# Gate and up slices in pairs of 1,024 columns, row gradients in one run per partition, and another issue order

## The chip, the cores and the metric

One core of a Trainium2 chip runs the kernel. It has five engines with a queue each: TensorE (PE), VectorE (DVE), ScalarE (ACT), GpSimd (POOL) and SyncE (SP). Sixteen DMA engines move data between device memory (DRAM) and the on-chip memory of 128 partitions; here nearly all transfers are issued by SP. The metric is the device time in microseconds (us); the time before is the median of three runs.

## The reference

A decode step of a transformer block, forward and backward: attention over a cache and a gated MLP side by side, and the gradients of all their inputs. All tensors are bf16.

```python
def _A_ref(x, k_cache, v_cache, wq, wo):          # B=2, Sq=1, D=576, Hq=32, Hkv=16, Sk=4096, Dh=128
    ...
    scores = jnp.einsum("bhqd,bhkd->bhqk", q, k) * (Dh ** -0.5)
    p = _softmax(scores, axis=-1)
    o = jnp.einsum("bhqk,bhkd->bhqd", p, v)
    return (lambda x, *d: x.transpose(*d))(o, 0, 2, 1, 3).reshape(B, Sq, Hq * Dh) @ wo

def _B_ref(x, w_gate, w_up, w_down):              # F = 4608
    g = jnp.einsum("bsd,df->bsf", x, w_gate)
    u = jnp.einsum("bsd,df->bsf", x, w_up)
    h = g * u
    return jnp.einsum("bsf,fd->bsd", h, w_down)

xn = _layernorm(x, axis=-1)
return x + _A_ref(xn, A_k_cache, A_v_cache, A_wq, A_wo) + _B_ref(xn, B_w_gate, B_w_up, B_w_down)
...
_out, _vjp = jax.vjp(_f, A_x, A_k_cache, A_v_cache, A_wq, A_wo, B_w_gate, B_w_up, B_w_down)
_grads = _vjp(grad_out)
```

The outputs are out_0 (the block's result), out_1 (gradient of x), out_2 and out_3 (of the K and V caches), out_4 (wq), out_5 (wo), out_6 (gate), out_7 (up), out_8 (w_down). With two rows of x, each weight and cache element is read once and each gradient element written once, and every gradient is an outer product of few vectors.

## The kernel before

**Work.** Attention runs in 16 steps (8 groups of two K/V heads, two batches). A step loads K and V of two heads, 1 MB each (128 partitions x 8 KB), transposes them on DVE in 32x32 blocks (`turn`), computes scores and softmax on PE, ACT and DVE (`softmax`, `dscore`), contracts (`contract`), and forms the gradients of V (`out1`, to out_3) and K (`out0`, to out_2) in `head_outer`: outer products on PE into a PSUM tile `ps_o`, four casts by ACT or DVE (`cp`, lines 436 and 438) into a store slot, one store of 1 MB. Each group also loads a slice of wq and one of wo, and `group_back` writes their gradients. The MLP is cut into nine slices of `FS` = 512 of the 4,608 columns (`mlp`).

**Buffers.** Sixteen slots of 8 KB per partition (`big`) are shared by three users with a cap each: loaded K/V (`kv`, 8), transposed data (`X`, 13) and outgoing gradients (`st`, 4). Gate and up of one slice go into the one `gu` tile (9 x 512 columns: four row blocks of gate, four of up, and the last 64 rows of both). Five `ww` tiles hold slices of wq, wo and w_down. `tl` tiles hold the gradients of the last 64 of the 576 rows (tails).

**Transfers of a slice.** Gate and up each come as one transfer of 512 rows x 512 columns (line 1039: runs of 1,024 bytes) and one of the last 64 rows (line 1042), w_down in 4,608 bytes per partition (line 1046). The main gradients of gate and up (`cols_outer`, 512 KB, runs of 1,024 bytes) and wq go out likewise; those of w_down and wo (`rows_outer`, 576 KB) put row a·128+p on partition p, four runs of 1,152 bytes for each partition. A row unit is two matmuls (line 699), one for each of two row groups of 32, into the two banks of a `ps_o` tile.

**Order.** The whole program is generated ahead by a planner (`Order`). Each piece of work is a stream that asks for slots, engines and transfers with costs written into the source; the planner starts what can start first and breaks ties within a window (`SLACK`) by a priority from `pr`, which adds up the tables `PR`, `HEAD`, `TAIL` and `OFF` by name and step. `MLP_AT`, `WQ_AT` and `WO_AT` tell after which K/V load a weight load may be asked for. What runs on the chip is the resulting fixed order of instructions of each engine, with waits on semaphores where data or slots are needed; SP issues its transfers in that order too. At the end of the run `final_out` (lines 1345 to 1364) sums and stores out_0, and `final_dx` (lines 1376 to 1402) out_1.

Of the kernel before, what the change touches and what calls it, by code (L numbers as in the profile page):

```python
# [13 lines left out]
P = 128  # L14
# [282 lines left out]
NBIG, NGU, NWW, NBD = 16, 1, 5, 3  # L297
CAP = {"kv": 8, "X": 13, "st": 4}
OFF = {"mload": {2: 138.2, 8: 8.9}, "wload": {10: 3.1, 13: 2.1}, "BD1": {1: -144.5}, "out1": {4: 2.3, 6: -20.1,
       8: 2.5}, "W1": {4: 1.3, 7: -1.7}, "turn1": {4: -0.1, 5: -115.7, 11: -198.7}, "load": {1: 20.8, 10: -89.9,  # L300
       11: -16.3, 14: -4.1}, "front": {3: -111.8, 14: -87.3}, "turn0": {4: 6.0, 15: -118.8}, "con": {10: 3.3},
       "W0": {14: -1.6}, "back": {5: -15.0}}
MLP_AT = [0.93, 10.84, 15.91, 23.71, 30.89, 34.72, 45.87, 53.36, 60.85]
WQ_AT = [-1, 8, 16, 24, 32, 40, 48, 56]
WO_AT = [3, 7, 16, 26, 34, 40, 50, 58]
# [6 lines left out]
HEAD = {"turn0": -25.2, "turn1": -31.7, "att": -70.5, "dsc": 459.9, "con": 83.3, "out1": 26.9, "out0": 94.5,  # L312
        "front": 23.5, "back": -376.6, "W0": -16.3, "W1": 64.8, "BD1": 30.3, "BD0": 46.9, "conv": -75.9,
        "load": -114.3}
TAIL = {"turn0": 43.7, "turn1": 191.7, "att": 96.6, "dsc": 0.2, "con": -89.5, "conv": 36.8, "out1": -32.0,
        "out0": 229.2, "front": -529.0, "back": -358.1, "W1": 39.2, "BD1": -22.9, "BD0": -120.6, "load": 281.8}
PR = {"turn0": -84.8, "turn1": -109.1, "att": -681.0, "dsc": -731.0, "conv": 64.6, "con": -230.8, "out1": 1310.1,
      "out0": 250.5, "front": 164.9, "back": -70.9, "W0": -353.3, "W1": -31.6, "BD1": 442.2, "BD0": -91.5,
      "mlp": -130.5, "wout": -277.2, "store": 413.2, "load": 0.3, "wload": -718.4, "fin": 231.3, "const": 5.5,
      "mload": -58.3}  # L320
# [8 lines left out]
def kernel(  # L329
# [30 lines left out]
    G = 2  # L360
# [12 lines left out]
    HD2 = D // 2  # L373
    WB = 4 * FS + 256
# [277 lines left out]
    class Store:  # L652
        def __init__(self, n, out, prio):
            self.n, self.out, self.prio = n, out, prio

        def done(self):
            self.n -= 1
            if self.n == 0:
                yield SPAWN(self.out(), self.prio + PR["store"])

    def put(engine, parts, tag, slot, events=(), row=8192):
        def run():
            for j, (dst, src, nbytes) in enumerate(parts):
                yield DMA(engine, 0.36, nbytes, row)
                nc.sync.dma_start(dst, src)
            yield ("lrel", tag, slot)
            for e in events:
                yield SET(e)
        return run

    def unit(mms, pe, cols, ev, store, quad=None, kind="r"):
# [6 lines left out]
        yield from store.done()  # L678

    def cols_unit(A, rhs, st, off):  # L680
# [7 lines left out]
        def ev(e, o):  # L688
            cp(e, view(st[:], 0, P, off + 256 * A, [[P, 2], [FS, 4], [1, P]]),
               o[:].rearrange("p a (d f) -> p a d f", d=4))  # L690
        return mms, (0.213, 0.208), 1024, ev

    def rows_unit(j, lhs, st):
        A, k = divmod(j, 2)

        def mms(o):
            for aa in range(2):
                a = 2 * A + aa
                nc.tensor.matmul(o[:, aa, 0:HD2], lhsT=lhs(a), rhs=dyr[32 * a:32 * a + 32, k * HD2:(k + 1) * HD2],
                                 start=True, stop=True)  # L700
# [3 lines left out]
        return mms, (0.12, 0.052), D, ev  # L704

    def rows_outer(lhs, dst, p, events=()):
        i = yield ACQ("st")
        st = st_t[i]
        src = st[:, 0:FC * D].rearrange("p (h n) -> p h n", h=FC)
        store = Store(FC, put("SP", [(dst, src, 128 * FC * D * 2)], "st", i, events, 4608), p)  # L710
        for a in range(FC):
            yield SPAWN(unit(*rows_unit(a, lhs, st), store), p)

    def cols_outer(rhs, dst, p, events=()):
        i = yield ACQ("st")
        st = st_t[i]
        src = st[:, 0:4 * FS].rearrange("p (c n) -> p c n", n=FS)
        store = Store(2, put("SP", [(dst, src, 128 * 4 * FS * 2)], "st", i, events, 4096), p)
        for A in range(2):
            yield SPAWN(unit(*cols_unit(A, rhs, st, 0), store), p)  # L720

    def tail_outer(rhss, dsts, p, events=()):
        i = yield ACQ("tl")
        st = tl_t[i]
        nw = len(rhss)
        parts = [(d, st[64 * w:64 * w + 64, 0:FS], 64 * FS * 2) for w, d in enumerate(dsts)]
# [722 lines left out]
```

## Time and profile before

| | us |
|---|---|
| median of 3 runs | 485.66 |
| lowest, highest | 484.40, 486.44 |
| the profiled execution's own time | 484.63 |
| its span on the core (first to last instruction) | 482.8 |

The profile is a page about one execution. It gives for each engine the busy time and its share of the span, and for the DMA engines the packets (a packet is one contiguous run that one of the 16 engines moves), their bytes, and the time they took as a share of 16 engines' span. Packets may overlap a little, so a stretch can show a share slightly over 1. "PE" rows are matmuls and "PEld" rows weight loads; "128*32" is rows x columns of the array that a matmul occupies, and the shape after it is that of the moving data. A group row ends with the busy time and the mean of one in ns, and after the second bar with the idle time before them and what ended it. A row of stretches gives for each engine the busy time and the count, then the TensorE clock granted (1.00 is full), the DMA share and GB/s. "SPq" rows are the issues of transfers; their duration is that of issuing, not of moving.

### The profile page before, as it was taken

The numbers are of one execution on the slowest core, as the hardware profiler recorded it, in microseconds if no ns is written. First come the engines' busy times: TensorE is split into PE (matmuls) and PEld (weight loads), VectorE is DVE, ScalarE is ACT, GpSimd is POOL, SyncE is SP. The second block draws the span as 40 slices with busy tenths as digits, with TensorE's granted clock in tenths as the row PEclk, the third lists the DMA queues.
The fourth block names the chain that finished last, engine by engine and source line by source line (L and its number), as shares of the span: only waits on it lengthen the run. The fifth ranks groups of instructions, "written<-read, shape, count | busy, mean of one in ns | idle before, by whom it ended". The sixth has DMA issues, their size and how long they took to land.

```text
span 482.8 us, 14538 instructions
## 1 busy us (share of the span) xinstructions
PE 367.1 (76%) x6122; PEld 209.5 (43%) x6122; DVE 352.8 (73%) x667; ACT 345.9 (72%) x520; POOL 155.5 (32%) x220
## 2 busy tenths in 40 slices
PE   1447869877985998578797687856995878896986
PEld 1324535444452553245353353434452444443534
DVE  8679565996875888776857697768877777758672
ACT  6039279986876688667887788837875768896892
POOL 3140314563115403423414242253404451430600
PEclk9969585775665558777675579567565765757565
DMA  7999999999999999999999999999999999999985
GB/s 295 417 366 374 339 406 375 308 405 412 403 401 388 409 400 407 375 409 407 389 385 417 411 373 415 398 392 412 388 390 367 402 411 382 414 390 416 411 351 193
DMA packets 65266, 185.90 MB, mean 385 GB/s; under 512 B 4393, under 2 KB 47665, under 8 KB 48817
## 3 DMA queue, kind: packets, MB, share of 16 engines
q1 hardware_dynamic: 65192, 184.96, 99.2%
q8 instruction: 48, 0.79, 0.6%
q14 instruction: 18, 0.14, 0.1%
q10 hardware_dynamic: 8, 0.00, 0.0%
HBM read 92.48 MB, written 92.48 MB: 383 GB/s over the span
## 4 chain that ended last, share of the span: by engine, by line
DMA 58%; PE 17%; ACT 9%; DVE 8%; issue 4%; SPq 3%; DVEq 0%; ACTq 0%
DMA out_dram<-big 26%; DMA gu<-in_B_w_up_dram 12%; DMA gu<-in_B_w_gate_dram 9%; ACT big L436 8%; DMA ww<-in_A_wo_dram 7%; DVE big L432 5%; PE ps_o L1138 4%; DMA big<-in_A_v_cache_dram 3%; PE ps_m L1293 2%; PE ps_m L1116 2%; PE ps_m L779 2%; DMA ww<-in_B_w_down_dram 2%; SPq L1042 2%; DVE big L438 1%; PE ps_m L900 1%
## 5 line engine op out<-in xcount | busy, mean ns | idle before, releaser
L436 ACT CAST big<-ps_o 128x1024 bf16<-128x1024 f32 (+1 forms) x325 | 289.9, 961 | 39.0 <-PE ps_o L1138 28.8
L432 DVE STREAM_TRANSPOSE big<-big 128x1024 f32<-128x1024 f32 x128 | 153.6, 1222 | 16.0 <-DMA out_dram<-big 8.3
L1104 POOL TENSOR_TENSOR BD<-vr,mask 128x2048 bf16<-128x2048 bf16 x32 | 115.3, 3604 | 112.3 <-ACT vr L436 77.0
L438 DVE CAST big<-ps_o 128x1024 bf16<-128x1024 f32 (+1 forms) x51 | 56.0, 1097 | 10.2 <-PE ps_o L1138 4.1
L1116 PE MATMUL ps_m<-big,W 128*32 128x128 bf16 x2048 | 58.3, 279 | 4.5 <-POOL W L1081 1.7
L1138 PE MATMUL ps_o<-BD,pp 32*128 32x512 bf16 x256 | 50.6, 549 | 9.6 <-ACT big L436 6.4
L1116 PEld LDWEIGHTS <-W 128*32 128x32 bf16 x2048 | 46.6, 124 | 20.8 <-issue 16.4
L1138 PE MATMUL ps_o<-BD,dd 32*128 32x512 bf16 x256 | 46.5, 496 | 6.2 <-ACT big L436 5.3
L1081 POOL COPY W<-rep 32x16 bf16<-32x16 bf16 x128 | 24.6, 192 | 65.3 <-DVE rep L884 60.4
L636 POOL COPY wt<-wm 64x128 bf16<-64x128 bf16 (+1 forms) x34 | 8.9, 261 | 107.1 <-DVE wm L629 105.9
L432 DVE STREAM_TRANSPOSE big<-ww 128x1152 f32<-128x1152 f32 x25 | 34.1, 1365 | 7.6 <-DMA out_dram<-big 4.9
L1293 PE MATMUL ps_m<-big,pp 128*32 128x512 bf16 x256 | 31.4, 592 | 0.0
L761 PE MATMUL ps_m<-gu,xs 128*32 128x128 bf16 x360 | 11.1, 279 | 26.7 <-DMA gu<-in_B_w_gate_dram 17.3
L432 DVE STREAM_TRANSPOSE big<-gu 128x1024 f32<-128x1024 f32 x18 | 21.6, 1226 | 5.1 <-DMA out_dram<-big 5.1
L1293 PE MATMUL ps_m<-big,dd 128*32 128x512 bf16 x256 | 23.9, 457 | 1.0 <-DVE hb L785 0.7
L764 ACT COPY gs<-ps_m 128x256 f32<-128x256 f32 x9 | 3.5, 384 | 29.2 <-PE ps_m L761 29.2
L1138 PEld LDWEIGHTS <-pp 32*128 32x128 bf16 x256 | 11.1, 100 | 26.6 <-issue 22.9
L1138 PEld LDWEIGHTS <-dd 32*128 32x128 bf16 x256 | 10.7, 98 | 25.1 <-issue 18.3
L685 PEld LDWEIGHTS <-xnr 32*128 32x128 bf16 x416 | 15.9, 119 | 12.8 <-issue 12.0
L761 PEld LDWEIGHTS <-xs 128*32 128x32 bf16 x360 | 7.7, 121 | 30.9 <-DMA gu<-in_B_w_gate_dram 19.4
L685 PE MATMUL ps_o<-hb,xnr 32*128 32x128 bf16 x288 | 16.7, 281 | 3.4 <-ACT big L436 2.9
L766 DVE TENSOR_TENSOR hb<-gs,ps_m 128x128 bf16<-128x128 f32 x9 | 2.6, 285 | 19.8 <-ACT gs L764 19.8
(199 smaller groups left out, 513.2 us busy)
## 6 DMA issues: line engine op xcount, KB each, us to landing
out_dram<-big SPq DMA_DIRECT2D x64, 1024.0 KB, 12.2
big<-in_A_k_cache_dram SPq DMA_DIRECT2D x32, 1024.0 KB, 12.7
big<-in_A_v_cache_dram SPq DMA_DIRECT2D x32, 1024.0 KB, 11.9
out_dram<-big SPq DMA_DIRECT2D x26, 512.0 KB, 11.3
out_dram<-big SPq DMA_DIRECT2D x17, 576.0 KB, 8.9
ww<-in_B_w_down_dram SPq DMA_DIRECT2D x9, 576.0 KB, 8.3
ww<-in_A_wo_dram SPq DMA_DIRECT2D x8, 576.0 KB, 10.7
gu<-in_B_w_gate_dram SPq DMA_DIRECT2D x9, 512.0 KB, 15.3
```

Source lines behind the costliest of these rows:

```text
L432: nc.vector.transpose(out, in_)
L436: nc.scalar.copy(out, in_)
L438: nc.vector.tensor_copy(out=out, in_=in_)
L685: nc.tensor.matmul(o[:, aa, dc * P:(dc + 1) * P], lhsT=xnr[32 * a:32 * a + 32, dc * P:(dc + 1) * P], rhs=rhs(a), start=True, stop=True)
L761: nc.tensor.matmul(ug[32 * a:32 * a + 32, 1 - w, :], lhsT=xs[:, dc if dc < 4 else 4 + w, :], rhs=gu[:, FS * k + P * a:FS * k + P * (a + 1) ...
L779: nc.tensor.matmul(dh, lhsT=Wdy[:, e, 2 * k:2 * k + P], rhs=view(X[:], 0, P, 64 * k + e, [[D, FC], [2, 32]]), start=(k == 0 and e == 0), s ...
L1042: nc.sync.dma_start(gu[64 * w:64 * w + 64, 8 * FS:9 * FS], Wsrc[512:576, f0:f0 + FS])
L1081: nc.gpsimd.tensor_copy(view(W_t[t][w][:], 32 * a, 32, 6 + 8 * a, [[G * WW, 4], [WW, G], [1, 2]]), view(rep_t[grp[g]["qs"]][:], 32 * a, 32 ...
L1104: nc.gpsimd.tensor_tensor(BD_t[i][:], view(vr_t[v][:], 0, P, 0, [[0, 16], [1, Dh]]), view(mask16[:], 0, P, 0, [[1, 16], [0, Dh]]), ALU.mult)
L1116: nc.tensor.matmul(sc[32 * cq:32 * cq + 32, :], lhsT=view(W[:], 0, P, (be * G + l) * WW + 6 - 4 * c2 - 2 * l, [[1, 32]]), rhs=view(X[:], 0 ...
L1138: nc.tensor.matmul(o[:, k, :], lhsT=pr2[32 * c4:32 * c4 + 32, :], rhs=BD[32 * c4:32 * c4 + 32, 8 * l + 4 * h2:8 * l + 4 * h2 + 4, :], star ...
L1293: nc.tensor.matmul(ct[32 * j:32 * j + 32, :], lhsT=view(rT, 0, P, 4 * c + 2 * l, [[1, 32]]), rhs=kv_t[kvS[s][t][l]][:, Dh * c:Dh * (c + 4) ...
```

## The change

It does four things. (1) Gate and up are loaded for two slices at once, 1,024 columns, each weight into one slot of the shared ring (new user `G`, cap 2); the `gu` tile keeps only the 64-row tails. The ninth slice stays alone. The two slices of a pair are still computed one by one. (2) The main gradients of gate and up of a pair fill one store slot for each weight, half by half, and leave in one transfer of 1 MB. (3) The row gradients (w_down and wo) are laid out with rows 4p to 4p+3 on partition p: a run of 4,608 bytes per partition. For that a row unit takes 8 matmuls of 32x32 in place of 2 of 32x128. (4) The planner's numbers are new: `kv` 7 for 8, `X` 12 for 13, six `ww` tiles for five, another cost for some transfers, and new tables throughout, so nearly every engine's order differs. The order of SP's transfers, which can be read from the built programs, has 252 transfers for 276.

```diff
 def DMA(engine, cost, nbytes, row=8192):
-    packet = 0.0364 * row + 8.0
+    packet = 0.0364 * row + 8.7
...
-NBIG, NGU, NWW, NBD = 16, 1, 5, 3
-CAP = {"kv": 8, "X": 13, "st": 4}
+NBIG, NGU, NWW, NBD = 16, 1, 6, 3
+CAP = {"kv": 7, "X": 12, "st": 4, "G": 2}
...
-LM, LAG = 0.16, 1.39
+LM, LAG = 0.15, 1.75
...
-SLACK = {"PE": 0.1, "ACT": 0.11, "DVE": 0.43, "POOL": 0.47, "SP": 17.19}
+SLACK = {"PE": 0.08, "ACT": 0.3, "DVE": 0.46, "POOL": 24.94, "SP": 1554.58}
...
-    kv_t = X_t = st_t = tiles("big", NBIG, [P, NCH * Dh])
+    kv_t = X_t = st_t = G_t = tiles("big", NBIG, [P, NCH * Dh])
...
-    gu_t = tiles("gu", NGU, [P, 9 * FS])
+    gu_t = tiles("gu", NGU, [P, 2 * FS])
...
+    def put(dst, src, nbytes, row, tag, slot, ready):
+        yield WAIT(*ready)
+        for d, x in zip(dst, src):
+            yield DMA("SP", 0.36, nbytes, row)
+            nc.sync.dma_start(d, x)
+        yield ("lrel", tag, slot)
...
-    def rows_unit(j, lhs, st):
+    def rows_unit(j, t, st):
...
             for aa in range(2):
-                a = 2 * A + aa
-                nc.tensor.matmul(o[:, aa, 0:HD2], lhsT=lhs(a), rhs=dyr[32 * a:32 * a + 32, k * HD2:(k + 1) * HD2],
-                                 start=True, stop=True)
+                for q in range(4):
+                    nc.tensor.matmul(o[32 * q:32 * q + 32, aa, 0:HD2], lhsT=view(t, 32 * q, 32, 2 * A + aa, [[4, 32]]),
+                                     rhs=dyr[32 * q:32 * q + 32, k * HD2:(k + 1) * HD2], start=True, stop=True)
...
+    def rows_outer(t, dst, p, event):
         i = yield ACQ("st")
+        st, done = st_t[i], events(FC)
+        yield SPAWN(put([dst.rearrange("(p c) n -> p (c n)", c=FC)], [st[:, 0:FC * D]], 128 * FC * D * 2, 4608,
+                        "st", i, done), p + PR["store"])
+        for j in range(FC):
+            yield SPAWN(unit(*rows_unit(j, t, st), done[j]), p)
...
+    def cols_store(i, dst, width, done):
+        return put([dst.rearrange("(c p) n -> p c n", p=P)], [st_t[i][:, 0:4 * width].rearrange("p (c n) -> p c n", n=width)],
+                   128 * 4 * width * 2, 2 * width, "st", i, done)
...
+    def cols_half(sl, hh, w, rhs, p, event):
+        if hh == 0:
+            sl["st"][w] = i = yield ACQ("st")
+            dst = (out_6, out_7)[w][0:512, sl["f0"]:sl["f0"] + sl["width"]]
+            yield SPAWN(cols_store(i, dst, sl["width"], sl["done"][w]), p + PR["store"])
+            yield SET(sl["open"][w])
+        else:
+            yield WAIT(sl["open"][w])
+        done = sl["done"][w][2 * hh:2 * hh + 2]
+        for A in range(2):
+            yield SPAWN(unit(*cols_unit(A, rhs, st_t[sl["st"][w]], FS * hh, sl["width"]), done[A]), p)
...
+    def free_gu(sl):
+        yield WAIT(*sl["turned"])
+        for b in sl["G"]:
+            yield REL("G", b)
+        yield REL("gu", sl["gu"])
...
+                t, c0 = (main[w], width * dc + FS * hh) if dc < 4 else (gu, FS * hh)
                 for a in range(4):
...
+                                     rhs=t[:, c0 + P * a:c0 + P * (a + 1)], start=(dc == 0), stop=(dc == 4))
...
-        t32(pairs(X[:, 0:2048]), pairs(gu[:, 0:2048]))
...
+            t32(pairs(X[:, 2048 * w:2048 * (w + 1)]).rearrange("p (c n) -> p c n", c=4),
+                pairs(main[w][:, 0:4 * width]).rearrange("p (c n) -> p c n", c=4)[:, :, HFS * hh:HFS * (hh + 1)])
...
+            halves = range(2 * i, min(2 * i + 2, NFS))
+            f0, width = 2 * i * FS, FS * len(halves)
...
             for w, Wsrc in enumerate((B_w_gate, B_w_up)):
...
+                b = yield ACQ("G")
+                sl["G"].append(b)
+                yield DMA("SP", 0.4, 128 * 4 * width * 2, 2 * width)
+                nc.sync.dma_start(G_t[b][:, 0:4 * width].rearrange("p (c n) -> p c n", n=width),
+                                  Wsrc[0:512, f0:f0 + width].rearrange("(c p) n -> p c n", p=P))
+                yield DMA("SP", 0.36, 64 * width * 2, 2 * width)
+                nc.sync.dma_start(gu[64 * w:64 * w + 64, 0:width], Wsrc[512:576, f0:f0 + width])
```

More of the change, by code (lines that the diff above doesn't have):

```diff
@@ L315 @@
[L315 to L320, printed above, removed]
+HEAD = {"turn0": 358.0, "turn1": -88.8, "att": -420.1, "dsc": 372.9, "con": 241.2, "out1": -625.8, "out0": 80.7,
+        "front": 43.6, "back": 73.0, "W0": 584.4, "W1": -340.9, "BD1": 39.3, "BD0": 397.4, "conv": 284.3,
+        "load": 102.5}
@@ L650, in dxn, with unit @@
                                  start=(s == 0), stop=(s == St - 1))
[L652 to L671, printed above, removed]
+    def put(dst, src, nbytes, row, tag, slot, ready):
[4 more added lines that the diff above has]
+        yield ("lrel", tag, slot)
+    def unit(mms, pe, cols, ev, done, quad=None, kind="r"):
         i = yield ACQ("o")
@@ L677, in unit, with events, cols_unit @@
         yield REL("o", i)
-        yield from store.done()
-    def cols_unit(A, rhs, st, off):
+        yield SET(done)
+    def events(n):
+        return [Event() for _ in range(n)]
+    def cols_unit(A, rhs, st, off=0, width=FS):
         def mms(o):
@@ L740, in tail_outer, with mlp @@
         for A in range(2):
[L741 to L749 removed]
+            yield SPAWN(unit(*mk(A), done[A]), p)
+        yield WAIT(*done)
+        yield SET(event)
+    def free_gu(sl):
[3 more added lines that the diff above has]
+        yield REL("gu", sl["gu"])
+    def mlp(i, hh, sl, Lgu, Ld, wd_slot):
+        gu, wd = gu_t[sl["gu"]], ww_t[wd_slot]
+        main, width = [G_t[b] for b in sl["G"]], sl["width"]
         hs = yield ACQ("hb")
@@ L1144, in mk @@
             return mms, (0.213, 0.052), 1024, ev
-        def one(A, h2):
-            yield from unit(*mk(A, h2), store, A)
-            yield SET(done[2 * A + h2])
         for h2 in range(2):
             for A in range(2):
-                yield SPAWN(one(A, h2), pr(f"out{t}", s))
+                yield SPAWN(unit(*mk(A, h2), done[2 * A + h2], A), pr(f"out{t}", s))
     def outer(s, t, tag, slot, pr2):
```

144 lines of the change are left out of this document (73 added, 71 removed), and 11 rows, old and new, of the table OFF.

## The prediction

> **What bounds the kernel now.** I read the page first, then the busy time by stretches, the issue rows of SP, and the end of the run in order of time.
>
> ```profile
> span 482.8 us, 14538 instructions
> PE 367.1 (76%) x6122; PEld 209.5 (43%) x6122; DVE 352.8 (73%) x667; ACT 345.9 (72%) x520; POOL 155.5 (32%) x220
> ...
> DMA packets 65266, 185.90 MB, mean 385 GB/s; under 512 B 4393, under 2 KB 47665, under 8 KB 48817
> ...
> q1 hardware_dynamic: 65192, 184.96, 99.2%
> ...
> out_dram<-big SPq DMA_DIRECT2D x64, 1024.0 KB, 12.2
> big<-in_A_k_cache_dram SPq DMA_DIRECT2D x32, 1024.0 KB, 12.7
> big<-in_A_v_cache_dram SPq DMA_DIRECT2D x32, 1024.0 KB, 11.9
> out_dram<-big SPq DMA_DIRECT2D x26, 512.0 KB, 11.3
> out_dram<-big SPq DMA_DIRECT2D x17, 576.0 KB, 8.9
> ```
>
> The packets of SP's queue took 99.2% of sixteen engines' whole span, while no compute engine is above 76%. The kernel is bound by its transfers. Three quarters of the packets are under 2 KB, although the 128 K/V transfers of 1 MB (128 packets of 8 KB each) hold 134 of the 186 MB. So the time can fall in two ways: cheaper packets for the same bytes, or fewer moments with nothing to move. The next view gives both; its last two columns are the DMA share and GB/s.
>
> ```profile
> 5.00:15.00 10.00, 2.53 (x48) 1.51 (x48) 9.13 (x34) 4.33 (x7) 0.00 (x0) 1.00 1.02 426
> 27.50:29.50 2.00, 0.37 (x2) 0.10 (x1) 1.78 (x3) 0.60 (x2) 2.00 (x2) 0.54 1.10 304
> 47.00:49.00 2.00, 1.06 (x8) 0.94 (x9) 0.90 (x4) 1.11 (x4) 0.00 (x0) 0.79 1.04 360
> 58.00:60.50 2.50, 2.50 (x86) 1.58 (x76) 1.51 (x3) 1.73 (x3) 0.00 (x0) 0.92 1.09 348
> ...
> 3.00:483.00 480.00, 367.09 (x6122) 209.54 (x6122) 350.70 (x659) 344.52 (x519) 153.09 (x209) 0.67 1.00 387
> 38.00:54.00 16.00, 11.62 (x260) 8.28 (x250) 13.61 (x27) 11.47 (x20) 1.63 (x3) 0.82 0.92 342
> 72.00:98.00 26.00, 22.72 (x440) 14.31 (x441) 19.61 (x37) 23.75 (x35) 13.79 (x16) 0.63 0.98 347
> 458.00:470.00 12.00, 10.52 (x152) 4.41 (x150) 8.09 (x13) 11.21 (x15) 1.61 (x3) 0.64 0.90 349
> 476.00:483.00 7.00, 3.13 (x16) 1.54 (x14) 1.52 (x9) 0.41 (x1) 0.00 (x0) 0.50 0.14 43
> ```
>
> What each short stretch moves follows from the issues:
>
> ```profile
> 2.64 0.97 SPq L1005 DMA_DIRECT2D big<-in_A_k_cache_dram  x2
> ...
> 10.88 1.93 SPq L1039 DMA_DIRECT2D gu<-in_B_w_gate_dram  x1
> ...
> 17.36 15.12 DMA gu<-in_B_w_up_dram
> ...
> 39.06 8.79 SPq L665 DMA_DIRECT2D out_dram<-big  x5
> 48.35 1.80 SPq L665 DMA_DIRECT2D out_dram<-tl  x2
> ...
> 52.89 0.38 SPq L1039 DMA_DIRECT2D gu<-in_B_w_gate_dram  x1
> ```
>
> From 5 to 15 us the 1 MB K/V loads run: 426 GB/s with 8 KB packets. At 27.5 to 29.5 (the up weights land at 32.5) and 58 to 60.5 gate and up loads run in 1,024-byte rows: 304 and 348 GB/s. At 47 to 49 gradients are stored, in rows of 1,024 and 1,152 bytes: 360 GB/s. The engines are equally full in all four (share 1.02 to 1.10; packets overlap a little), so the rate falls with the row. Against that full share, three stretches ran partly dry: (1.02-0.92)x16 + (1.02-0.98)x26 + (1.02-0.90)x12 = 4.1 us. The last 7 us move almost nothing.
>
> **The packets, step by step.** The time of a packet on one of 16 engines is 16 x bytes / rate: 8,192 B take 307.7 ns; a 1,024 B load takes 47.1 (58 to 60.5) or 53.9 ns (27.5 to 29.5); a gradient packet of 1,024 B takes 45.5 ns, or, if all were 1,152 B, 51.2. Taking time = fixed + bytes x slope, the fixed part from the pair (8,192; 1,024) is (t - 307.7/8)/(7/8): 9.9 or 17.6 ns for loads, 8.0 to 9.2 for stores (the 1,152-byte pair likewise). The bytes do not change, so only the fixed part is saved, once per packet that goes away.
> - Gate, up and their main gradients: four pairs of slices, two weights; 1,024 packets become 512. 8 x 512 = 4,096 fewer in loads, 4,096 in stores. The ninth slice stays as it was.
> - The 64-row load tails of these pairs: 8 x 64 = 512 fewer. The tail stores stay.
> - Row gradients (the 17 stores of 576 KB above): 512 packets of 1,152 B become 128 of 4,608 B: 17 x 384 = 6,528 fewer.
>
> Loads 4,608 x 9.9 ns / 16 = 2.9 us, stores 10,624 x 8.0 / 16 = 5.3 us: **8.2 us**. Bounds: 7.6 us with 8.0 ns for all; 11.2 us with 17.6 and 9.2. I take the low ends because the 27.5 stretch has the highest overlap (1.10), so its price is partly a queue and not a packet. SP also issues 252 transfers in place of 276. At 16 end marks each (4,393 small packets / 276) that is 384 packets; at no more than the 8 ns fixed part, 0.2 us, left in the bounds.
>
> **What the edit adds.** Casts and transposes keep their number and elements; gate and up are now read in four runs per transpose. One wait grows: a pair's main gradient leaves SP after four casts, two from each half, where two were enough, and everything later in SP's order stands behind it.
>
> ```profile
> SPq L665 <- ACT big L436: 88.7, 53, 7.4
> ```
>
> SP waits 88.7 us for casts already, 7.4 at the longest, and the engines stay full, because transfers land 11 to 13 us after their issue and so some 4 MB are queued. A longer wait costs what it exceeds that cover; it is in the order's term below. The row gradients get new matmuls: 8 of 32x32 per unit where 2 of 32x128 stood, 68 units.
>
> ```profile
> L699 PE MATMUL ps_o<-dyr,R 32*128 32x288 bf16 x64 | 10.6, 376 | 2.7 <-ACT big L436 2.2 <-DVE big L438 0.3
> L699 PE MATMUL ps_o<-dyr,hb 32*128 32x288 bf16 x72 | 10.0, 335 | 4.8 <-ACT big L436 4.3 <-DVE big L438 0.2 <-DVE tl L438 0.2
> ...
> L1310 PE MATMUL ps_m<-fold,osb 128*128 128x4 bf16 x128 | 8.4, 170 | 3.1 <-ACT osb L1303 2.8
> ```
>
> A unit occupies PE for (10.6+10.0)/68 = 0.30 us now. A matmul with 4 columns lasts 0.17 us, so of 0.335 to 0.376 some 0.19 us is streaming. If four row groups run side by side, as two do now, a unit makes two rounds: about +0.2 us, 14 us over the run, inside PE's 116 us of idle time. If all eight take turns, a unit makes eight streams: +1.1 us. No row of before has four row groups writing one bank, so this stands between +0.2 and +1.1; I take +0.2 (L699 itself overlaps its two) and keep the other as a rival.
>
> **The order.** Both programs' issue orders can be read before they run, and they differ nearly everywhere. Three things bear on time.
> - The end. After the last row-gradient work, before runs out_0 and then out_1's chain on PE, one behind the other:
>
> ```profile
> 472.40 0.32 DVE L973 TENSOR_TENSOR accx<-accx,ps_m 128x160 f32<-128x160 f32 x1
> ...
> 472.83 1.87 PE L1359 MATMUL ps_o<-identf,acc 128*2 128x64 f32 x16
> 474.62 0.37 PE L1362 MATMUL ps_o<-identf,acc 64*2 64x64 f32 x2
> ...
> 480.21 0.41 ACT L1337 CAST xy<-ps_o 2x320 bf16<-2x320 f32 x1 [4.77 <-PE ps_o L1400]
> ```
>
> The new order has out_0's 18 matmuls ahead of the last evictions and the L643 group ahead of the last column unit. From 472.26 to 474.99 that is 2.7 us out of the chain that ends the run. The four row units at the end give back 4 x 0.2 = 0.8. Together **-1.9 us**, between 0 (the last store decides instead) and -2.7.
> - The gaps. They could all be filled (-4.1). Against that stand new long bursts: the longest row of stores without a load is 9.1 MB (before 5.5), and a dry queue is more likely there, because a 1 MB store needs four casts of some 1.03 to 1.21 us:
>
> ```profile
> L436 ACT CAST big<-ps_o 128x1024 bf16<-128x1024 f32 x270 | 259.7, 1026 | 32.2 <-PE ps_o L1138 28.8 <-PE ps_o L685 1.8 <-DMA out_dram<-big 1.0
> ...
> L438 DVE CAST big<-ps_o 128x1024 bf16<-128x1024 f32 x38 | 46.1, 1214 | 6.4 <-PE ps_o L1138 4.1 <-ACT big L436 0.7 <-PE ps_o L685 0.6
> ```
>
> With ACT and DVE both at it and nothing else to do, that is 4/(1/1.026+1/1.214) = 2.2 us a MB against 2.46 at 426 GB/s; any transpose in between makes casts the limit. An open pair holds two input slots and two of the four store slots until its second half is done. I take **+2.0 us**, half of today's gaps; bounds -4.1 and +8.2 (three times today's gaps).
> - K/V loads have 7 of the shared slots, not 8; that risk is in the same bound.
>
> Sum on the profiled execution: its time is 484.6 us (span 482.8 and 1.8 around it); 484.6 - 8.2 - 1.9 + 2.0 = 476.5. The median of before's runs is 1.0 above that execution, so **477.5 us** for the median.
>
> **The rivals.**
> - *The last V load becomes the bound (slower).*
>
> ```profile
> 426.51 0.33 SPq L1005 DMA_DIRECT2D big<-in_A_v_cache_dram  x1
> ```
>
> From this last load's issue to the end are 482.8 - 426.5 = 56.3 us. Behind it the queue of before holds 16.7 MB, the new one 12.4: it is issued 4.3 MB later, 11.1 us at 387 GB/s. Were the chain behind it (transposes, scores, last stores, row gradients, final sums) no shorter, the end would move by 11.1 less the some 7.6 us saved by then: 485.7 + 3.5 = 489 us. For it: ACT is busy 11.2 of 12 us from 458 to 470. Against: the new order casts the last slice's gradients before this chain and takes out_0 out of it. It decides once the chain needs more than about 48 us.
> - *Row groups take turns in a PSUM bank (slower).* Then 68 units cost +1.1 us each, 75 us of the 116 idle. The last four lengthen the tail by 4.4 in place of 0.8 us, and if a tenth of the others' 70 us is not covered: 477.5 + 3.6 + 7 = 488 us. Against: matmuls of different row groups overlap in L699, though into two banks.
> The Trainium skill speaks for this rival: "TensorEngine Tiling (Array Packing)", Gotcha 1, says different row tiles cannot use one PSUM bank at once. By that rule the sum would be the 488 just given; no row of before shows such a case.
> - *Row length isn't what slows the small rows.* The DRAM step between gate and up rows, 9,216 bytes, stays. Were the step or the load itself the cause, no packet would be worth its fixed part and the change would not do what it says: 477.5 + 8.2 = 485.7, within 0.5%. Against: row gradients go to a contiguous region and still run at 360.
> The Trainium skill has a rule of this kind, in "DMA: Bandwidth & Descriptors", Specifications: full rate from 512 B on. By it the sum would be 485.7; the 360 against 426 GB/s above speaks against it.
> - *The order is better than taken.* Gaps filled: 477.5 - 2.0 - 4.1 = 471.4.
>
> **How the numbers follow.** Within 0.5% (483.2 to 488.1) this kernel's measurement can't tell a change. Chances: forecast 0.63 (472 to 483.2), better order 0.10, row length 0.06, turns in a bank 0.07, last V load 0.14. The first two are faster, 0.73; row length and a third of the slower two (they straddle 488.1) are no change, 0.13; the rest slower, 0.14. The low end comes from filled gaps with part of the higher packet price, 470.5; the high end reaches into the slower two, 488.
>
> **What would show it.** The packet count should be about 49,600 (65,266 - 15,232 - 384), with the same bytes. Stretches with gate and up loads should run near 16 x 2,048/(47.1+38.5) = 383 GB/s, and the mean over the busy span near 394. L715 (the old L699) at 0.5 us a unit shows row groups side by side; over 1 us, turns. In the last 7 us out_0's matmuls should be gone. I am wrong if the packets fall and the mean rate doesn't, or if DMA shares under 0.95 take more than 10 us in all.

## The result, and the profile after

The changed kernel takes **482.85 us** (median of 14 runs, 481.72 to 484.53) against 485.98 for the kernel before (14 runs beside it). The ratio is 0.9945, 95% interval 0.9926 to 0.9963: 2.7 us faster (1.8 to 3.6), where 8.2 were forecast. Ratios below are against runs of the kernel before on the same chip; 0.001 is 0.49 us. A difference between two changed kernels is the difference of their ratios; taking the two intervals together by squares, it is uncertain by 1.2 to 1.9 us either way.

The page of the kernel after, its span, engines, packets and SP's queue:

```profile
span 481.7 us, 15312 instructions
...
PE 386.8 (80%) x6530; PEld 217.9 (45%) x6530; DVE 360.0 (75%) x667; ACT 343.2 (71%) x520; POOL 155.4 (32%) x220
...
DMA packets 49652, 185.94 MB, mean 386 GB/s; under 512 B 4008, under 2 KB 21168, under 8 KB 33200
...
q1 hardware_dynamic: 49576, 184.96, 98.0%
```

The packets fell from 65,266 to 49,652, as counted beforehand, and the bytes are the same. But the mean rate went only from 385 to 386 GB/s, which with equal bytes says the same as the span; the prediction named this as its refutation. Its second sign came too: the DMA share is far under 0.95 for 24 us in all, 12 of them new (33 to 45 us). Five stretches tell where the saving went. Each row has the engines' busy times, and at its end the granted TensorE clock, the DMA share and GB/s; first the kernel before, then the kernel after:

```profile
3.00:33.00 30.00, 10.34 (x184) 7.50 (x188) 22.43 (x65) 8.68 (x19) 8.45 (x25) 0.91 1.02 394
33.00:45.00 12.00, 10.26 (x220) 5.47 (x212) 10.46 (x17) 10.59 (x14) 0.00 (x0) 0.80 0.98 372
45.00:455.00 410.00, 324.43 (x5475) 185.97 (x5475) 303.20 (x549) 308.51 (x465) 140.56 (x181) 0.65 1.02 394
455.00:471.00 16.00, 14.34 (x194) 5.76 (x191) 11.48 (x18) 14.63 (x20) 4.07 (x3) 0.61 0.93 360
471.00:483.00 12.00, 7.72 (x68) 4.84 (x67) 3.13 (x13) 2.11 (x4) 0.00 (x0) 0.50 0.51 183
```

```profile
3.00:33.00 30.00, 14.55 (x315) 11.64 (x316) 22.83 (x69) 11.30 (x25) 4.89 (x24) 1.00 1.02 381
33.00:45.00 12.00, 10.27 (x232) 7.30 (x235) 11.41 (x23) 8.50 (x11) 0.57 (x2) 0.58 0.74 268
45.00:455.00 410.00, 339.80 (x5731) 187.72 (x5723) 310.28 (x541) 305.40 (x462) 147.07 (x181) 0.66 1.01 399
455.00:471.00 16.00, 15.00 (x190) 7.10 (x184) 10.54 (x17) 12.81 (x16) 0.46 (x2) 0.61 1.00 402
471.00:483.00 12.00, 7.23 (x77) 4.14 (x76) 2.81 (x12) 3.76 (x6) 0.00 (x0) 0.50 0.32 119
```

- **The middle gains.** From 45 to 455 us the rate is 399 for 394 GB/s: 5 x 410 = 2.05 MB more, some 5.1 us at 399 (rounding of the two rates leaves about 1 us either way).
- **The front loses.** By 45 us the kernel after has moved (394-381) x 30 + (372-268) x 12 = 1.64 MB less, 4.1 us. From 33 to 45 us its DMA engines run dry, share 0.74.
- **The tail** still moves little in its last 12 us (share 0.32). The span ends 1.1 us earlier, which agrees with 5.1 - 4.1 within that rounding.

Why the front runs dry is seen on SP of the kernel after, in its issues:

```profile
33.02 0.35 SPq L681 DMA_DIRECT2D out_dram<-big  x1
37.01 1.15 SPq L681 DMA_DIRECT2D out_dram<-tl  x2
38.80 0.33 SPq L1044 DMA_DIRECT2D big<-in_A_v_cache_dram  x1
```

and in the longest of its waits from 24 to 46 us (in all, times, longest):

```profile
SPq L681 <- ACT big L461: 14.7, 3, 10.3
```

SP stood 10.3 us on the casts of the first MLP gradient (out_8, issued at 33.02) and then on those of its tails (37.01). The next K/V load, at 38.80, stands behind them in SP's order. In the kernel before, the last load ahead of the first store (the one at 39.06) is this one on SP:

```profile
32.24 0.96 SPq L1005 DMA_DIRECT2D big<-in_A_k_cache_dram  x1
```

The row units have these two groups in the kernel after (matmuls, their count, busy time and mean ns of one):

```profile
L715 PE MATMUL ps_o<-dyr,R 32*32 32x288 bf16 x256 | 18.1, 396 | 2.1 <-ACT big L461 1.1
L715 PE MATMUL ps_o<-dyr,hb 32*32 32x288 bf16 x288 | 16.1, 337 | 1.1 <-DVE tl L463 0.5
```

(18.1 + 16.1) / 68 = 0.50 us a unit. The four matmuls that write one bank start together: the first four of the run all between 29.53 and 29.54 us.

### The profile page after: what moved, and what is told of

Read it like the earlier page. It is cut to its first block, busy times and chain, and to the rows that moved or that the text cites. A ratio compares the mean times of both kernels' runs of the same rounds, so it can differ in the third digit from the quotient of the medians.

```text
span 481.7 us, 15312 instructions
## 1 busy us (share of the span) xinstructions
PE 386.8 (80%) x6530; PEld 217.9 (45%) x6530; DVE 360.0 (75%) x667; ACT 343.2 (71%) x520; POOL 155.4 (32%) x220
## 2 busy tenths in 40 slices
DMA packets 49652, 185.94 MB, mean 386 GB/s; under 512 B 4008, under 2 KB 21168, under 8 KB 33200
## 4 chain that ended last, share of the span: by engine, by line
DMA 46%; PE 30%; ACT 10%; DVE 7%; issue 4%; SPq 3%; DVEq 0%; ACTq 0%
DMA out_dram<-big 29%; ACT big L461 8%; PE ps_o L1183 6%; PE ps_m L1335 5%; DMA big<-in_A_k_cache_dram 5%; DMA big<-in_A_v_cache_dram 5%; PE ps_m L1162 4%; DVE big L457 3%; DMA ww<-in_B_w_down_dram 3%; PE ps_o L715 3%; DMA ww<-in_A_wo_dram 2%; PE ps_m L941 2%; DVE big L463 2%; DMA ww<-in_A_wq_dram 1%; PE ps_o L701 1%
## 5 line engine op out<-in xcount | busy, mean ns | idle before, releaser
L461 ACT CAST big<-ps_o 128x1024 bf16<-128x1024 f32 (+1 forms) x319 | 283.0, 955 | 41.0 <-PE ps_o L1183 22.1
L457 DVE STREAM_TRANSPOSE big<-big 128x1024 f32<-128x1024 f32 x146 | 175.8, 1223 | 23.9 <-DMA out_dram<-big 17.0
L463 DVE CAST big<-ps_o 128x1024 bf16<-128x1024 f32 (+1 forms) x57 | 66.4, 1166 | 12.8 <-PE ps_o L1183 4.3
L1183 PE MATMUL ps_o<-BD,dd 32*128 32x512 bf16 x256 | 51.4, 527 | 7.5 <-ACT big L461 5.5
L1335 PE MATMUL ps_m<-big,dd 128*32 128x512 bf16 x256 | 28.8, 540 | 9.8 <-DVE dd L457 4.7
L715 PE MATMUL ps_o<-dyr,R 32*32 32x288 bf16 x256 | 18.1, 396 | 2.1 <-ACT big L461 1.1
L461 ACT CAST osb<-ps_m 128x512 bf16<-128x512 f32 x16 | 9.6, 598 | 12.7 <-PE ps_m L1335 9.3
L941 PE MATMUL ps_m<-big,Wdy 128*128 128x128 bf16 x144 | 15.4, 292 | 3.4 <-DVE cr L1287 1.8
L715 PE MATMUL ps_o<-dyr,hb 32*32 32x288 bf16 x288 | 16.1, 337 | 1.1 <-DVE tl L463 0.5
L941 PEld LDWEIGHTS <-Wdy 128*128 128x128 bf16 x144 | 13.8, 134 | 6.3 <-issue 6.3
## 6 DMA issues: line engine op xcount, KB each, us to landing
ww<-in_B_w_down_dram SPq DMA_DIRECT2D x9, 576.0 KB, 12.4
```

The source lines that it names most:

```text
L457: nc.vector.transpose(out, in_)
L461: nc.scalar.copy(out, in_)
L463: nc.vector.tensor_copy(out=out, in_=in_)
L715: nc.tensor.matmul(o[32 * q:32 * q + 32, aa, 0:HD2], lhsT=view(t, 32 * q, 32, 2 * A + aa, [[4, 32]]), rhs=dyr[32 * q:32 * q + 32, k * HD2: ...
L941: nc.tensor.matmul(dp, lhsT=Wdy[:, e, 2 * k:2 * k + P], rhs=view(X[:], 0, P, 64 * k + e, [[D, GH], [2, 32]]), start=(k == 0 and e == 0), s ...
L1183: nc.tensor.matmul(o[:, k, :], lhsT=pr2[32 * c4:32 * c4 + 32, :], rhs=BD[32 * c4:32 * c4 + 32, 8 * l + 4 * h2:8 * l + 4 * h2 + 4, :], star ...
```

## The experiments

**Which part of the packets pays.** Each kernel here takes back, or adds alone, one part of the change; all else, with the order of the engines, stays.

*Long row gradients in the order of before*: the kernel before, with 8 small matmuls a unit and one run of 4,608 bytes per partition.

```diff
-        src = st[:, 0:FC * D].rearrange("p (h n) -> p h n", h=FC)
+        src = st[:, 0:FC * D]
...
-                                out_8[f0:f0 + FS, :].rearrange("(a p) n -> p a n", p=P), po, (E[0],)), po)
+                                out_8[f0:f0 + FS, :].rearrange("(p c) n -> p (c n)", c=FC), po, (E[0],)), po)
```

> The kernel before with its own order; only the row gradients (17 stores) leave in 4,608-byte runs with the eight small matmuls. Theory A (packets are worth their fixed part of about 8 ns each, the new order lost the rest): 6,528 fewer packets x 8 ns / 16 = 3.3 us less, 482.7 us, ratio 0.993, and the fed DMA stretches gain it. Rival B (longer runs are worth a third of that or less, the new order is neutral): at most 1.2 us less, ratio 0.9975 or above.

Measured: 484.48 us, ratio 0.9962 (0.9937 to 0.9987), so 1.8 us gained (0.6 to 3.1): between the two theories.

*Short row gradients in the new order*: the same, taken back from the kernel after.

> The changed kernel with its own order; only the row gradients go back to 1,152-byte runs and two matmuls a unit. Theory A: 3.3 us more than the changed kernel's 482.85, 486.1 us. Rival B: about 1 us more, 484 us.

Measured: 485.09 us, ratio 0.9975 (0.9955 to 0.9995): 1.5 us over the kernel after, between the two again. The row gradients are worth 1.5 to 1.8 us, half of the 6,528 x 8.0 / 16 = 3.3 that the prediction gave them.

*Short pairs in the new order*: main loads and main gradients of gate and up in two transfers of 512 columns each (the loads are shown; the gradients are split likewise).

```diff
-                nc.sync.dma_start(G_t[b][:, 0:4 * width]..., Wsrc[0:512, f0:f0 + width]...)
+                for h in range(len(halves)):
+                    nc.sync.dma_start(G_t[b][:, 4 * FS * h:4 * FS * (h + 1)]..., Wsrc[0:512, f0 + FS * h:f0 + FS * (h + 1)]...)
```

> The changed kernel with its own order; only the pairs' main transfers (gate, up and their gradients) go in two transfers of 512 columns each, so in 1,024-byte runs, 8,192 more packets and 16 more issues. Theory A: 4,096 x 9.9 ns / 16 + 4,096 x 8.0 ns / 16 = 4.6 us more, 487.4 us. Rival B: 1 to 2 us more, 484.4 us.

Measured: 485.37 us, ratio 0.9995 (0.9974 to 1.0017): 2.4 us over the kernel after, where the predicted price made 4.6.

*Both short in the new order*: nothing is left of the change but the order, the slots and the 64-row load tails of the pairs (512 packets fewer).

> The changed kernel's order with the old run lengths of rows and pairs: what the order alone does. Theory A: 482.85 + 3.3 + 4.6 = 490.7 us, so the order alone is 4.8 us slower than before (ratio 1.010). Rival B: 485.5 us, so the order alone is neutral.

Measured: 488.29 us, ratio 1.0059 (1.0034 to 1.0085). This lies halfway between the two theories, and two things follow. All long rows together are worth 1.0059 - 0.9945, or 5.5 us (1.5 either way), more than the 1.5 and 2.4 one by one, but within their uncertainty. And the new order by itself is 2.9 us (1.7 to 4.1) *slower* than the old one.

*Loads or stores of the pairs alone.*

> The changed kernel in its own order, where only the loads of the gate and up pairs go out as two transfers of 512 columns (runs of 1,024 bytes; 8 x 512 = 4,096 more packets, 8 more issues); the gradient stores keep runs of 2,048 bytes. With loads and stores both short the kernel took 2.5 us more. Theory L (a load's run of 2,048 bytes costs as much as two of 1,024, only stores pay for packets): at most 0.7 us over the changed kernel, 482.9 to 483.6. Theory P (the prediction's 9.9 ns a load packet): 4,096 x 9.9 / 16 = 2.5 us over it, 485.4. Between 0.7 and 1.8 the two directions share the saving.

Measured: 484.51 us, ratio 0.9964 (0.9948 to 0.998): 0.9 us over the kernel after.

> The changed kernel in its own order, where only the main gradients of the gate and up pairs go out as two transfers of 512 columns (runs of 1,024 bytes; 4,096 more packets, 8 more issues); the loads keep runs of 2,048 bytes. Theory L (only stores pay for packets): 1.8 to 2.5 us over the changed kernel, 484.7 to 485.4. Theory P (8.0 ns a store packet as predicted, and 9.9 a load packet): 4,096 x 8.0 / 16 = 2.0 us, 484.9, with the loads' run 2.5 us over as well. If both runs stay under 1 us, the 2.5 us of the run with both short came from its 16 more issues or from chance.

Measured: 484.87 us, ratio 0.9981 (0.9964 to 0.9999): 1.8 us over it. The two add up to 2.7, beside the 2.4 above. The loads gain less than the 2.5 of the predicted price; the stores, 1.8, fit the 2.0 of theirs. But each is uncertain by 1.2 us, so that the loads' gain is not clear of nothing, and neither theory has the split shown. So the prices were measured by themselves.

*Transfers alone*: the shapes of this kernel on SP's queue, one kind after the other, in one execution.

> All computation is left out; what stays are transfers of this kernel's shapes on SP's queue, one kind after the other, each long enough for a stretch of its own: loads of 8,192-byte rows, gate and up loads in rows of 1,024 and then 2,048 bytes; stores of 8,192 bytes, of 1,024 and 2,048 (columns), of 1,152 and 4,608 bytes (row gradients); then 8,192-byte stores taking turns with K/V loads, with gate and up loads of 1,024 and of 2,048 bytes. Theory P (time = fixed + bytes x slope, 8 to 10 ns fixed a packet, as the prediction had it): loads 345 and 383 GB/s, stores 360 and 390, 360 and 411 against 426, and the mixed stretches in between in the same way (about 382 with 1,024 and 404 with 2,048). Theory L (a longer load row saves nothing): the two gate and up load stretches within 3% of each other, the store stretches apart by 6% or more.

The stretches of that run (DVE and POOL busy times, then the clock, the DMA share and GB/s). In order: loads of 8,192-byte rows, gate and up loads of 1,024 and of 2,048; stores of 8,192, column stores of 1,024 and 2,048, row gradients of 1,152 and 4,608; then 8,192-byte stores in turn with K/V loads, with loads of 1,024 and with loads of 2,048:

```profile
9.00:25.00 16.00, 0.41 (x1) 0.00 (x0) 1.00 1.01 424
30.00:46.00 16.00, 0.00 (x0) 0.00 (x0) 1.00 1.10 348
54.00:72.00 18.00, 0.00 (x0) 0.00 (x0) 1.00 1.05 386
77.00:91.00 14.00, 0.00 (x0) 0.00 (x0) 1.00 1.01 427
95.00:102.00 7.00, 0.00 (x0) 0.00 (x0) 1.00 1.09 386
105.00:111.00 6.00, 0.00 (x0) 0.00 (x0) 1.00 1.05 409
114.00:124.00 10.00, 0.00 (x0) 0.00 (x0) 1.00 1.07 378
127.00:139.00 12.00, 0.00 (x0) 0.00 (x0) 1.00 1.03 415
147.00:177.00 30.00, 0.00 (x0) 0.00 (x0) 1.00 1.01 428
182.00:218.00 36.00, 0.00 (x0) 0.00 (x0) 1.00 1.06 400
226.00:258.00 32.00, 0.00 (x0) 0.00 (x0) 1.00 1.03 418
```

With 16 x bytes / rate for a packet's time, one packet fewer saves:
- loads: 2 x 47.1 - 84.9 = 9.3 ns, where 9.9 was predicted;
- column stores: 2 x 42.4 - 80.1 = 4.8 ns, where 8.0 was;
- row gradients: (4 x 48.8 - 177.7) / 3 = 5.8 ns, where 8.0 was.

The theory that a longer load row saves nothing is refuted: 348 and 386 are 11% apart. Measured alone, a load packet has the price that was predicted, and a store packet 28% (row gradients) to 40% (columns) less. With these prices the packet term is 4,608 x 9.3 / 16 + 4,096 x 4.8 / 16 + 6,528 x 5.8 / 16 = 2.7 + 1.2 + 2.4 = 6.3 us. The runs with short rows leave out the 512 tail packets, 0.3 us of it; the other 6.0 lie inside the 5.5 us with its 1.5 of uncertainty. Kind by kind it fits less well: for the pairs the runs have 0.9 for the loads, where these prices make 2.4, and 1.8 for the stores, where they make 1.2.

**The front.** *Eight K/V slots in steps 0 to 2* (of the 16 shared ones), seven from step 3 as in the kernel after. The sequence of SP's transfers then differs from that of the kernel after only around the first MLP gradients: one V load now stands ahead of them, and two K loads and a slice each of wq and wo come before the pair's main gradients.

```diff
             yield PRIO(pr("load", s))
+            if s == 0:
+                od.cap["kv"] = 8
+            if s == 3:
+                od.cap["kv"] = 7
```

> The changed kernel, with eight slots for K/V in place of seven in the first three steps: SP's order changes in rows 19 to 32 only (a V, two K loads and a wq and wo slice go ahead of the first gradients' stores), later rows differ in slot numbers alone. Theory F (the dry stretch from 34 to 41 us, share 0.54, is SP waiting for the first MLP gradients with no load allowed): the stretch 33 to 45 us goes from 268 GB/s to 370 or more, and the time falls by 2.5 to 3.5 us, 479.4 to 480.4 us. Rival G (what is gained at the front is waited for later, since the end hangs on the last V load's chain or on casts): the stretch fills, but the time falls by less than 1 us.

Measured: 480.55 us (9 runs), ratio 0.9913 (0.9885 to 0.9941). The stretch that ran dry, in this run:

```profile
33.00:45.00 12.00, 7.40 (x204) 5.22 (x201) 9.62 (x19) 7.39 (x10) 0.34 (x2) 0.79 0.95 364
```

364 GB/s for 268: the dry stretch came from the loads that stood behind the waiting stores. The ratio is 1.6 us below that of the kernel after, with overlapping intervals, and between the two theories. Two more pairs below, each the same kernel with and without this edit, differ by 1.7 and 1.1 us in the same direction. So the front is worth some 1 to 2 us of time, less than the 4.1 us of bytes. Why the medians show less is open. In the profiled executions it is not given back: this run's casts on ACT start 3 to 4.5 us earlier than those of the kernel after nearly all the way from 140 us on, and the span falls by 3.8 us, 481.7 to 477.9. But that execution was the fastest of the nine and does not stand for the median.

**The tail.** *out_0 last*: the priority of the final sums put back, so that out_0's matmuls stand at the end as in the kernel before.

```diff
-"fin": -292.2
+"fin": 931.3
```

> The changed kernel, but out_0's sums and store and out_1's chain get the lowest rank, so out_0's 18 matmuls come behind the last row unit, column units and tails again, as before the change; the rest of the order is the same up to SP's row 242 of 246. Theory C (the end is one chain on PE from the last V load on; moving out_0 within it gains nothing): 482.85 us within 0.8. Rival D (the prediction's term: out_0 ahead of the last evictions takes 1.9 to 2.7 us out of the end): 484.8 to 485.5 us.

Measured: 483.07 us, ratio 0.9965 (0.9938 to 0.9993): 1.0 us over the kernel after, uncertain by 1.6. The move itself brings no gain clear of noise, where the prediction's sum had 2.7.

*Front and out_0 together.*

> The version with eight K/V slots in steps 0 to 2 (480.55 us, 2.3 less than the changed kernel) and out_0 left for the end (within 0.8 us of the changed kernel by itself) together. If the tail's serial PE work is the same wherever out_0 stands: 480.0 to 481.2. If the few 0.1 us that the run with out_0 last showed in its favour (span 480.0 against 481.7) are real and add: 479 to 480.

Measured: 482.59 us (6 runs), ratio 0.993 (0.9903 to 0.9957), 1.7 us below out_0 last by itself. The expectation is missed. Against the front edit alone, at 0.9913, it is 0.8 us slower, again not clear of noise. The two comparisons together, 0.9 us with some 1.2 either way, leave no room for 2.7.

*The eighth slot from step 14 on*, meant to bring the last V load earlier, and *the eighth slot at both ends*:

> The changed kernel, with eight slots for K/V in place of seven from step 14 on: the order of SP is the same up to row 205 of 246, then the last V load has 18.7 MB queued behind it in place of 12.4. Theory C (the last V load sets the end; the transfers run dry in the last 12 us because the chain behind it is longer than what is queued): the stretch from 471 us on loses its low DMA share and the time falls by 1.5 to 3 us, 480 to 481.3 us. Rival E (the tail costs what it cost before the change, the new order loses at the front only): 482.85 us within 0.8.

> Both of the two edits with eight K/V slots, at the front and from step 14 on. Theories C and F together: their gains add, 477 to 479 us, near the 477.5 us that was predicted for the change. Rivals: no more than the better one of the two alone.

Measured: 499.29 us, ratio 1.0294 (1.0261 to 1.0327), and 498.18 us, ratio 1.0265 (1.0232 to 1.0298). Neither theory expected this. The slot comes out of the shared ring of 16, which transposed data and outgoing gradients need too, and the whole tail is planned anew. A stretch of the first run:

```profile
455.00:471.00 16.00, 14.02 (x256) 7.35 (x256) 13.61 (x23) 13.55 (x20) 5.45 (x2) 0.79 0.66 258
```

and SP's waits in it from 395 to 500 us:

```profile
SPq L681 <- ACT big L461: 23.8, 10, 7.1
SPq L681 <- DVE big L463: 21.3, 7, 6.9
```

Stores wait 45 us for casts, and the DMA share falls to 0.66. As the whole tail differs, that tells neither the price of a slot by itself nor what the last V load is worth. So one transfer was moved by itself.

*The last V load ahead of three stores, and with the last K and V loads ahead of five.* Only SP's order changes; the stores follow behind the load.

```diff
-            nc.sync.dma_start(d, x)
+            held.append((d, x)) if nput[0] in LATER else nc.sync.dma_start(d, x)
...
                     nc.sync.dma_start(kv_t[i][:], views[t][b, G * g + l])
+                    while n == 4 * NS - 1 and held:
+                        nc.sync.dma_start(*held.pop(0))
```

> The changed kernel with one thing moved on SP: the last V load is issued ahead of the three stores that stood just before it (out_5 of 576 KB, out_4 of 512 KB and its tail, 1.2 MB together), which follow behind it; all other engines keep their order. Theory V (the chain behind this load, 33.3 us from its landing without a gap, sets the end): 1.2 MB less ahead of it let it land some 2.9 us earlier, and the end comes 1.5 to 2.9 us earlier, 480.0 to 481.4. Theory S (other work is as late, and the load is last on the chain only by a little): less than 0.7 us, 482.2 or more.

Measured: 484.86 us, ratio 0.9991 (0.9967 to 1.0015): 2.2 us *slower* than the kernel after.

> The same with the two out_2 stores of 1 MB before them held back too: the last K load, the last two V loads go ahead of 3.3 MB of stores; the last V load could land some 8 us earlier. Theory V: 3 to 6 us off the changed kernel, 477 to 480, limited by the 6.9 us that the tail now runs dry. Theory S: within 0.7 us, or slower, since the held stores keep four slots longer.

Measured: 487.66 us, ratio 1.0049 (1.0021 to 1.0076): 5.1 us slower than it. Neither theory expected that much. In the kernel after, the chain of waits goes from the last V load to the end without a gap, by way of out_0's matmuls (start, us, what):

```profile
432.59 15.80 DMA big<-in_A_v_cache_dram
...
469.30 1.80 PE ps_o L1401 x16
```

DVE transposes behind that load, in order of time (in brackets what it waited for):

```profile
444.28 1.25 DVE L457 STREAM_TRANSPOSE big<-big 128x1024 f32<-128x1024 f32 x1 [0.49 <-DMA out_dram<-big]
448.42 1.25 DVE L457 STREAM_TRANSPOSE big<-big 128x1024 f32<-128x1024 f32 x1 [0.25 <-DMA big<-in_A_v_cache_dram]
```

The transpose that was held 0.49 us by a store, in the kernel with three stores moved back:

```profile
447.72 1.25 DVE L457 STREAM_TRANSPOSE big<-big 128x1024 f32<-128x1024 f32 x1 [3.21 <-DMA out_dram<-big]
```

And the casts of a 1 MB gradient in the one with five moved back:

```profile
442.03 1.93 ACT L461 CAST big<-ps_o 128x1024 bf16<-128x1024 f32 x2 [6.53 <-DMA out_dram<-big]
442.04 1.23 DVE L463 CAST big<-ps_o 128x1024 bf16<-128x1024 f32 x1 [5.68 <-DMA out_dram<-big]
```

What waits here waits for a *store to land*, because it writes into the slot that the store reads. In the kernel after the V load ends last on the chain, but the slots of the stores ahead of it come free only just before they are needed. With three stores moved back the last V load lands 2.2 us earlier (446.2 us for 448.4). Set against the kernel after, instruction by instruction, this run is 0.7 us late on DVE just before that transpose, 3.4 us at it, and still 2.4 us at the end. With five moved back the casts on ACT run 1.4 us ahead until this wait and 4 to 6 us behind after it, 2.9 at the end. So the delay enters where a slot's store has not landed, and it is more than the earlier load brings.

*The same with the better front.*

> The version with eight K/V slots in steps 0 to 2 (480.55 and, with out_0 last, 482.59: 0.4 to 2.3 us under the changed kernel) with the same five stores held back behind the last V load. Theory V: the two gains add, 475 to 478.5. Theory S: as without, 480.5 to 482.5.

Measured: 487.26 us, ratio 1.0027 (1.0005 to 1.005): 1.1 us better than without the front's slot; both theories are missed, that of the sum of two gains by far.

*Without most of out_0's matmuls.*

```diff
-                if dc < 4:
+                if dc == 3 and k == 1:
```

> The changed kernel without seven of the eight matmul calls that add up out_0 (14 of the 16 rows of the L1401 group, 1.87 us for 16, so some 1.6 us of PE), which leaves that output incomplete; every engine keeps its order. Theory C (the end is one serial chain on PE, in which out_0's matmuls stand wherever they are put): 1.2 to 1.6 us less, 481.2 to 481.7. If it is under 0.5 us, PE had slack at that place and the chain of waits only passes through it.

Measured: 483.11 us, ratio 0.995 (0.993 to 0.9969): nothing gained, 0.2 us over the kernel after (1.3 either way): in line with the expectation's last case, slack on PE at that place. The last issues of SP, first in the kernel after, then in this one:

```profile
475.98 0.47 SPq L681 DMA_DIRECT2D out_dram<-tl  x1
479.58 0.26 SPq L1383 DMA_DIRECT2D out_dram<-xy  x1
```

```profile
473.01 0.48 SPq L681 DMA_DIRECT2D out_dram<-tl  x1
476.61 0.26 SPq L1383 DMA_DIRECT2D out_dram<-xy  x1
```

and the group of the last tail store among the issues after 465 us, whose last figure is the time from issue to landing, in the same order:

```profile
out_dram<-tl SPq DMA_DIRECT2D x1, 64.0 KB, 4.1
```

```profile
out_dram<-tl SPq DMA_DIRECT2D x1, 64.0 KB, 6.4
```

PE's chain is done 3.0 us earlier (out_1 is issued at 476.61 for 479.58). Half of that, 1.5 us, this execution was ahead before it came to out_0's matmuls; the other 1.5 are what they cost PE. But the tail store lands at 473.01 + 6.4 = 479.4 for 475.98 + 4.1 = 480.1, which fits a queue that is fuller 3 us earlier. The span shrinks by 1.2 us, from 481.7 to 480.5, which is less than that lead, and the median not at all. Two ends lie within 2 us of each other: PE's chain and the last bytes of the queue.

## Why the prediction was wrong, step by step

The sign was right and the range held the time, but the gain is a third of the forecast. Against the sum (-8.2 packets, -1.9 tail, +2.0 order, together -8.1) the runs show -5.5 for the long rows and +2.9 for the order with its tail, together -2.6 (they add up because both come from one run, the one with both short). So two steps failed, each by some 2.7 us: the packet term, whose price for stores was too high, and the tail's gain, which was to cancel the order's loss and did not. That the range held the time is no proof of the sum: its bounds were wide, those of the order's term alone from -4.1 to +8.2.

- **Packets: right mechanism, the store term mis-sized.** The count was right, the load price measured alone too (9.3 ns for 9.9; gate and up loads run at 386 GB/s for a predicted 383). The 8.0 ns of a store packet are 4.8 and 5.8: alone, the old rows run at 386 and 378 GB/s, not 360. Stores were two thirds of the term, so 5.3 us became 3.6. The prediction read the 360 off one 2 us stretch at 47 us with two kinds of store in it and took it as the price of all. Its first 0.7 us, mostly row gradients, ran at 373 GB/s, near the 378 alone; the column stores behind them ran at 350 (49.0 to 50.5 us), and at 348 in the other run with the old order (48.5 to 50.5). In the run that has short pair stores in the new order, column stores of the same 1,024-byte runs go at 384 (47.0 to 50.5), as they do alone. So 350 is not the price of that row length; what slowed them there is open. The lower bound of 7.6 us rested on the same row, so it could not catch this. By kind the matter is less settled than in sum, as the runs with loads or stores of the pairs alone show: there the loads, not the stores, fell short of their price.
- **Row length isn't what slows small rows: refuted.** All four pairs of stretches, alone and mixed, are faster with the longer row; the row gradients are the cleanest pair, with equal transfers and only the run changed (378 and 415 GB/s). The Trainium skill, "DMA: Bandwidth & Descriptors", Specifications, which has full rate from 512 bytes on, does not agree with these: 348, 386 and 424 GB/s for loads of 1,024, 2,048 and 8,192 bytes.
- **The tail, -1.9: not borne out.** out_0's matmuls did leave the last 7 us (they start at 469.30 on the chain, 12.4 before the end), and it gained nothing clear of noise. Put back, they cost 1.0 and 0.8 us in two comparisons, where 2.7 was counted; left out, they gain nothing. The prediction counted all of a serial stretch of PE as the run's end, and did not ask when the last bytes would land; its bound "0, the last store decides instead" is what the run without them shows.
- **The order, +2.0: sign right, and its place now known in part.** The new order costs 2.9 us by itself. By bytes that is a loss at the front, part of it made good later: the profile with both short is 1.77 MB (4.5 us) behind the kernel before by 45 us, loses about 1 us more up to 455 us, and gains 0.8 MB (2.0 us) from 455 to 471. Of the front's loss some 1 to 2 us come back when a K/V load no longer stands behind stores that wait for casts, with eight slots for K/V in place of seven. The prediction put that smaller share in one bound and did not look for its place. Whether the rest could be had back is open.
- **The last V load as the bound: not as put.** It is last on the chain, and from its issue to the end take 481.7 - 432.6 = 49.1 us, just over the 48 at which the rival was to decide. (The prediction's own figures give 44.7 for that limit: the span of 474.7 that it forecast less an issue at 426.5 + 11.1 - 7.6 = 430.0; 49.1 is over both.) But moved ahead it makes the end later. The waits shown point to the ring of slots: stores, casts, transposes and loads wait for one another in turn. Whether a V load that costs no other transfer its place would help was not tried.
- **Turns in a PSUM bank: refuted.** 0.50 us a row unit is the +0.2 taken, and four matmuls into one bank start within 0.01 us. By "TensorEngine Tiling (Array Packing)", Gotcha 1, of the Trainium skill it would have been near 1.4 us; this trace does not agree.

The version with eight K/V slots in the first three steps is the best measured: 480.55 us, ratio 0.9913 (0.9885 to 0.9941) to the kernel before; its interval overlaps that of the kernel after.

## What to carry to other kernels

Price a packet from stretches that hold one kind of transfer and nothing else, loads and stores apart, and from more than one: the same column stores ran at 350 GB/s in one order and at 384 in another. If the profile has only one, the bounds must allow for that. When an order is made anew, count the bytes moved by the first few tens of microseconds, and look on the transfer queue for a load behind a store that waits for compute. Before work taken off the end of a chain is counted as gain, ask when the last byte would land without it; and in a ring of slots, ask which store's landing a moved transfer delays.

## What the runs showed of the hardware

Alone on the queue, short rows cost loads more than stores: 1,024-byte rows ran at 348 GB/s in and 386 out, while 8,192-byte rows ran at 424 in, 427 out and 428 in turn. Where the loads kept the engines full, the DMA share rose as the rate fell (1.10 at 348, 1.01 at 424), so a full share says nothing about the rate. Alone, column stores in 1,024-byte runs, 9,216 bytes apart in memory, were no slower (386) than row gradients of 1,152 bytes in one piece of memory (378): the step did not count here. Inside the kernel such column stores ran at 350 GB/s in the old order and at 384 in the new one; no run shows why.
